# Order and issuing engine of the first loads in a fused spectral-filter and GEGLU kernel

## The chip, the core and the metric

The kernel runs on one core of one Trainium2 chip. The metric is the device time of one execution in microseconds (us); lower is better. Before the change it is 1331.72 us, the median of three runs (1331.66 to 1331.9).

## What is computed

A gate mixes two branches over 2048 tokens of 576 features. Branch A is a 2-D FFT over tokens and features, a product with a complex filter, and the inverse transform. Branch B is a GEGLU layer with 4608 hidden features. All is float32.

```python
x = A_x                                                   # 1 x 2048 x 576
g = sigmoid((x * gate_w).sum(-1, keepdims=True))
a = irfft2(rfft2(x, axes=(-2, -1)) * (w_r + 1j * w_i), s=(2048, 576), axes=(-2, -1))
h = gelu(x @ w_gate, approximate=True) * (x @ w_up)       # 2048 x 4608
b = h @ w_down                                            # 2048 x 576
out = g * a + (1 - g) * b
```

## The kernel before

**Tiling.** The tokens are cut into two halves (p = 0, 1) of 1024, each of two blocks (tb = 0, 1) of 512. The hidden features are 36 tiles of 128 (index j); tile j has a gate part (s = 0) and an up part (s = 1). The 576 input features are contracted in five slices k = 0..4; slice 4 holds the last 64 features twice, in a form of its own. Every float32 product is made of three products of rounded parts: high weight by high x, low weight by high x, high weight by low x. So each slice of x and of the weights is first copied by ScalarE into its high part (the helper `copy`, line 239), and VectorE then subtracts to get the low part. Slice 4 of x needs a copy and two VectorE operations with a mask `msk` (helper `stacked`, lines 243 and 244).

**What order the work has.** The schedule is manual: the instructions of each engine run in the order in which the Python code emits them. Functions `chain` (one tile, one block, one part: 14 matmuls on 512 columns) and `down_mm` (288 columns, the down projection) emit the matmuls; `gap` is called between them and emits a little VectorE and ScalarE work from queues (`aux`, `later`, `gens`), paced by a credit in us. Most of the kernel after the first tiles computes two tiles and two blocks together with seven block products (functions `products` and `seven`, line 1290); the spectral branch runs on VectorE, ScalarE and, for its column transforms, TensorE beside that.

**The start.** Six matmuls on a tile of zeros (`idle`, line 1458) run on TensorE while the first loads are under way. Then `first_chains` (line 879) computes tiles j = 0 and 1 of block tb = 0 together, slice by slice as the loads come in: for k = 0, 1, 2 six matmuls for j = 0 (into `px`) and six for j = 1 (into `pgu`), then slices 4 and 3 of j = 0, then slices 4 and 3 of j = 1. That makes 56 matmuls. After them `chain` runs block tb = 1 of the same two tiles (lines 859 to 866).

The names in the profile: `til<-xt` are loads of x slices, 256 KB each, five for tb = 0 (called xa[0] to xa[4] below; entries 0 to 4 of the list `x0` in the code) and five for tb = 1 (xb[0] to xb[4]; entries 5 to 9 of that list). `low<-wgu` of 128 KB is one slice of the weights of one tile (w0[k] for j = 0, w1[k] for j = 1). `low<-wd` (288 KB) are down weights of one tile. `xraw<-xs` and `tmp<-xs` (256 KB) are quadrants of x for the seven-product part, `rows<-xn` (2304 KB) the rows for the spectral branch and the gate, `low<-gw` the gate vector. `xhi`, `xlo`, `xtl` are the parts of x, `gub` the parts of the gate and up weights, `gl` and `hb` the activations.

**Who asks for what.** SyncE (SP) and GpSimd (POOL) issue the loads. SP asks for the x slices, for w0[0] and w1[0], the mask, xb, the first two down weights, the first four quadrants, the gate vector, the rows and four more quadrants, in this order; POOL asks for the other eight weight slices. Completion of SP's DMAs is counted by eight semaphores used in turn, so each DMA of SP waits until the one eight places ahead of it has landed.

ScalarE's order at the start is: for each k the weight slice of j = 0, the x slice (for k = 0 VectorE makes it), the weight slice of j = 1; then xb[0], xb[1], xb[2]; then the GELU of tile 0 (line 897); then xb[3] and xb[4]; then the GELU of tile 1. VectorE's order follows it: the low parts of xb[0] to xb[2] (line 789), the product of tile 0 (line 904), the low part of xb[3], the two mask operations on xb[4] (lines 243, 244).

```python
for k in (0, 1, 2, 4, 3):
    for j, w in ((0, w0), (1, w1)):
        g = gu_of(j)
        copy(g[:, 0, k], w[:, k])
        ...
        vec.tensor_tensor(g[:, 1, k], w[:, k], f(g[:, 0, k]), ALU.subtract)
        if j == 0 and 0 < k < 4:
            copy(xhi[0][:, k], x0[k])
```

Of the kernel before, what the change touches and what calls it, by code (L numbers as in the profile page):

```python
# [24 lines left out]
KT = 5  # L25
# [150 lines left out]
def _build(nc, tc, a):  # L176
    with ExitStack() as ctx:
# [3 lines left out]
        vec, act, pl, pe = nc.vector, nc.scalar, nc.gpsimd, nc.tensor  # L181

        def mk(n, shape, dt=F32):
            return pool.tile([P] + shape, dt, name=n, tag=n)

        def f(x):
            return x.bitcast(F32)
# [14 lines left out]
        raw = [low[:, i * (KT * 256 + D):(i + 1) * (KT * 256 + D)] for i in range(2)]  # L202
        hb = [mk(f"hb{i}", [2, TB], F32R) for i in range(3)]
        gl = [mk(f"gl{i}", [TB]) for i in range(2)]
        xraw = mk("xraw", [4, TB])
# [6 lines left out]
        msk = mk("msk", [2 + 96])  # L212
# [25 lines left out]
        def copy(o, i):  # L238
            act.activation(o, i, AF.Copy)  # L239
# [546 lines left out]
        def prep_x(tb, k, src):  # L786
            if k < 4:
                copy(xhi[tb][:, k], src)
                vec.tensor_tensor(xlo[tb][:, k], src, f(xhi[tb][:, k]), ALU.subtract)
                credit[0] -= 0.7  # L790
            else:
                copy(xtl[tb], src)
                stacked(xtl[tb], src)
                credit[0] -= 1.45

        def gu_of(j):
            return gub[gu_at(j)].rearrange("p (l t k) -> p l t k", l=2, t=KT)
# [281 lines left out]
        def load_xs(p, i, quads):  # L1079
            for q in range(4):  # L1080
                nc.sync.dma_start(quads[q], a["xs"][p, q // 2, q % 2][:, i])
# [353 lines left out]
        w0, w1 = (raw[j][:, 0:KT * 256].rearrange("p (t k) -> p t k", t=KT) for j in range(2))  # L1435
        w0d, w1d = (a["wgu"][j].rearrange("p (t k) -> p t k", t=KT) for j in range(2))
        for k in (0, 1, 2, 4, 3):
            nc.sync.dma_start(x0[k], a["xt"][0][:, k, 0:TB])
            (pl if k else nc.sync).dma_start(w0[:, k], w0d[:, k])
            (pl if k else nc.sync).dma_start(w1[:, k], w1d[:, k])  # L1440
        nc.sync.dma_start(msk, a["msk"])
        for k in range(KT):
            nc.sync.dma_start(x0[5 + k], a["xt"][0][:, k, TB:2 * TB])
        for i in range(2):
            nc.sync.dma_start(raw[i][:, KT * 256:], a["wd"][i])
        load_xs(0, 0, [xraw[:, q] for q in range(4)])
        nc.sync.dma_start(gwb, a["gw"][0:1, :].to_broadcast([P, D]))
        load_rows(0)
        load_xs(0, 1, [tmp[:, D + TB * q:D + TB * (q + 1)] for q in range(4)])
# [1 line left out]
        idle = hb[2][:, 0]  # L1451
# [4 lines left out]
        ps = ps_gu()  # L1456
        for _ in range(6):
            pe.matmul(ps, idle[:, 0:P], idle, start=True, stop=True)
        for k in (0, 1, 2, 4, 3):
            for j, w in ((0, w0), (1, w1)):  # L1460
                g = gu_of(j)
                copy(g[:, 0, k], w[:, k])
                if j == 0 and k == 0:
                    vec.tensor_copy(xhi[0][:, k], x0[k])
# [3 lines that stand above are left out]
                if j == 0 and k < 4:  # L1468
                    vec.tensor_tensor(xlo[0][:, k], x0[k], f(xhi[0][:, k]), ALU.subtract)
                elif j == 0:  # L1470
                    prep_x(0, k, x0[k])
# [150 lines left out]
```

## Time and profile before

| | |
|---|---|
| time, median of 3 runs | 1331.72 us |
| the profiled execution's own time | 1331.82 us |
| its span, first to last instruction | 1330.1 us |
| TensorE matmul busy | 1320.0 us, 99% of the span |
| VectorE busy | 1163.7 us, 87% |
| ScalarE busy | 873.0 us, 66% |
| GpSimd busy | 277.4 us, 21% |
| mean DMA rate over the span | 186 GB/s |
| DMA rate in the first fortieth of the span (33 us) | 354 GB/s |

Times in the views are us from the start of the span. A line of a timeline gives the start, the length, the engine (PE is TensorE's matmuls, DVE VectorE, ACT ScalarE, SPq the issuing of a DMA by SyncE), the source line, the operation, written and read tile, the count where equal instructions are merged, and in brackets the idle time before it with what ended it. A line of windows gives a stretch, its length, the busy time of each engine with the number of instructions, the granted TensorE clock, the busy share of the 16 DMA engines and the bytes moved in GB/s. In the lines on DMA queues, q1 is the queue of SyncE and q0 that of GpSimd.

### The profile page before, as it was taken

To read this page: it belongs to the slowest core of one execution; us is meant where nothing else is said; L and a number is where in the kernel's file an instruction comes from. 1 tells how busy PE (TensorE), PEld (TensorE's weight loads), DVE (VectorE), ACT (ScalarE), POOL (GpSimd) and SP (SyncE) were. 2 spreads that over 40 slices of the span, in tenths; PEclk is the share of its full clock that TensorE was granted. 3 is DMA by queue.
4 is the path that set the end of the run, shared out by engine and by line. 5 is a ranking of instruction groups with operands and counts; after the bars stand their busy time and mean duration, and the time that the engine had idled before them with its cause. 6 is when DMAs were issued, how large, how long until landed. Compare 5 with 4: busy or idle time off the path is not lost.

```text
span 1330.1 us, 20238 instructions
## 1 busy us (share of the span) xinstructions
PE 1320.0 (99%) x7294; PEld 1167.6 (88%) x7294; DVE 1163.7 (87%) x1653; ACT 873.0 (66%) x1583; POOL 277.4 (21%) x350
## 2 busy tenths in 40 slices
PE   9999999999999999999999999999999999999998
PEld 7888888888888888888888898888888888888887
DVE  7789999978999997975789988899999969999854
ACT  5686765665657557787578787647575686576562
POOL 1011221221212212112302231211222242222241
PEclk9999999999999999999999999999999999999999
DMA  9346677797777777999978998677777798676796
GB/s 354 135 115 128 130 135 136 156 267 164 148 153 139 150 155 183 280 236 287 277 235 214 239 237 193 125 252 220 155 148 147 157 258 179 136 142 127 183 195 178
DMA packets 108693, 247.57 MB, mean 186 GB/s; under 512 B 12848, under 2 KB 17840, under 8 KB 106800
## 3 DMA queue, kind: packets, MB, share of 16 engines
q0 software_dynamic: 46752, 97.34, 44.4%
q1 hardware_dynamic: 61840, 148.93, 34.1%
q8 instruction: 57, 0.93, 0.3%
q14 instruction: 44, 0.36, 0.1%
HBM read 133.88 MB, written 109.95 MB: 183 GB/s over the span
## 4 chain that ended last, share of the span: by engine, by line
PE 95%; ACT 2%; DVE 1%; issue 1%; DMA 0%; SPq 0%; DVEq 0%; ACTq 0%
PE pdn L943 33%; PE px L1290 20%; PE pgu L1290 20%; PE px L1292 3%; PE pgu L1292 3%; PE pgu L859 3%; PE pgu L860 3%; PE pgu L861 3%; PE pdn L304 1%; PE px L304 1%; ACT til L239 1%; PE px L860 1%; PE px L861 1%; PE px L859 1%; PE pgu L865 1%; PE pgu L866 1%
## 5 line engine op out<-in xcount | busy, mean ns | idle before, releaser
L956 POOL DMA_DIRECT2D yd<-stg x264 | 226.8, 862 | 953.8 <-ACT stg L975 894.3
L975 ACT ACTIVATE stg<-pdn,omg 128x576 f32<-128x576 f32 x276 | 204.8, 743 | 334.8 <-PE pdn L943 203.8
L943 PE MATMUL pdn<-dn,hb 128*128 128x288 f32 x1572 | 231.1, 294 | 0.1
L943 PEld LDWEIGHTS pdn<-dn,hb 128*128 128x128 f32 x1572 | 221.7, 188 | 9.5 <-ACT stg L975 0.7
L1277 DVE TENSOR_TENSOR gub<-low,gub 128x768 fp32r<-128x768 f32 x124 | 118.2, 953 | 8.4 <-ACT gub L1274 7.0
L1290 PE MATMUL pgu<-xhi,gub 128*128 128x512 f32 x392 | 122.0, 392 | 0.6 <-ACT px L239 0.6
L1290 PE MATMUL pgu<-til,gub 128*128 128x512 f32 x420 | 107.4, 391 | 0.0
L943 PE MATMUL pdn<-dn,ext 128*128 128x288 f32 x672 | 106.7, 294 | 0.0
L943 PE MATMUL pdn<-dn,gub 128*128 128x288 f32 x672 | 106.5, 294 | 0.0
L239 ACT ACTIVATE gub<-low 128x512 fp32r<-128x512 f32 (+2 forms) x147 | 97.7, 666 | 13.4 <-DVE low L1267 6.4
L943 PEld LDWEIGHTS pdn<-dn,ext 128*128 128x128 f32 x672 | 98.0, 188 | 4.1
L943 PEld LDWEIGHTS pdn<-dn,gub 128*128 128x128 f32 x672 | 97.8, 188 | 4.0
L1290 PEld LDWEIGHTS pgu<-til,gub 128*128 128x128 f32 x420 | 77.0, 188 | 14.5
L1290 PE MATMUL px<-xhi,gub 128*128 128x512 f32 x280 | 86.9, 391 | 0.0
L1290 PE MATMUL px<-til,gub 128*128 128x512 f32 x336 | 86.0, 391 | 0.0
L1290 PEld LDWEIGHTS pgu<-xhi,gub 128*128 128x128 f32 x392 | 70.8, 188 | 13.3 <-ACT px L239 1.1
L943 PE MATMUL pdn<-dn,hx 128*128 128x288 f32 x516 | 82.3, 296 | 0.0
L1267 DVE TENSOR_TENSOR low<-low 128x768 f32<-128x768 f32 x81 | 77.3, 955 | 0.8
L1290 PE MATMUL pgu<-xlo,gub 128*128 128x512 f32 x196 | 76.3, 389 | 0.0
L859 PE MATMUL pgu<-xhi,gub 128*128 128x512 f32 x192 | 75.1, 391 | 0.0
L860 PE MATMUL pgu<-xhi,gub 128*128 128x512 f32 x192 | 75.0, 391 | 0.0
L861 PE MATMUL pgu<-xlo,gub 128*128 128x512 f32 x192 | 74.9, 390 | 0.0
(278 smaller groups left out, 2968.9 us busy)
## 6 DMA issues: line engine op xcount, KB each, us to landing
yd<-stg POOLq DMA_DIRECT2D x264, 288.0 KB, 5.1
low<-ws SPq DMA_DIRECT2D x94, 384.0 KB, 4.8
gub<-wd SPq DMA_DIRECT2D x56, 288.0 KB, 3.9
low<-wgu SPq DMA_DIRECT2D x13, 640.0 KB, 7.1
rows<-col POOLq DMA_DIRECT2D x32, 256.0 KB, 5.9
gub<-ws SPq DMA_DIRECT2D x18, 384.0 KB, 5.2
lo<-dn SPq DMA_DIRECT2D x18, 288.0 KB, 2.7
dn<-lo POOLq DMA_DIRECT2D x18, 288.0 KB, 5.1
```

Source lines behind the costliest of these rows:

```text
L239: act.activation(o, i, AF.Copy)
L304: pe.matmul(v[al][:, :NK], c[:, al, q], two(x)[:, al], start=n == 0, stop=n == 2)
L859: pe.matmul(ps, w[:, 0, k, c], xhi[tb][:, k], start=k == 0, stop=False)
L860: pe.matmul(ps, w[:, 1, k, c], xhi[tb][:, k], start=False, stop=False)
L861: pe.matmul(ps, w[:, 0, k, c], xlo[tb][:, k], start=False, stop=False)
L943: pe.matmul(ps[half], h[:, l, c], d[:, q, half * HD:(half + 1) * HD], start=part == 0 and n == 0, stop=part == 1 and n == 2)
L956: pl.dma_start(yd[u], o, accum_op=ALU.add)
L975: at(n, lambda: put(u, lambda o: act.activation(o.rearrange("p (c k) -> p c k", c=2), v[:, :, 0:HD], AF.Copy, scale=omg[:, u:u + 1]), i == 0))
L1267: vec.tensor_tensor(o, p, q, ALU.subtract)
L1277: vec.tensor_tensor(w[:, 0:5:2], x, f(w[:, 1:4]), ALU.subtract)
L1290: pe.matmul(ps, l, x[:, t], start=first and t == 0 and q == 0, stop=False, skip_group_check=True)
L1292: pe.matmul(ps, w[:, 512 + P * s:512 + P * (s + 1)], xt, start=False, stop=True, skip_group_check=True)
```

## The change

Only the first loads change. SP now asks for the whole of what tiles 0 and 1 of block tb = 0 need, slice by slice: xa[k], w0[k], w1[k] for k = 0, 1, 2, then the mask, then slices 4 and 3; after them the xb slices, the gate vector, the rows and the second four quadrants. GpSimd no longer asks for weight slices. It sets 16 columns of the tile of zeros to zero once more, which makes it wait until the six matmuls on that tile have read it, and then asks for the two down weights and the first four quadrants, which SP asked for before. No instruction of TensorE, VectorE or ScalarE is added, removed or moved.

```diff
         for k in (0, 1, 2, 4, 3):
             nc.sync.dma_start(x0[k], a["xt"][0][:, k, 0:TB])
-            (pl if k else nc.sync).dma_start(w0[:, k], w0d[:, k])
-            (pl if k else nc.sync).dma_start(w1[:, k], w1d[:, k])
-        nc.sync.dma_start(msk, a["msk"])
+            nc.sync.dma_start(w0[:, k], w0d[:, k])
+            nc.sync.dma_start(w1[:, k], w1d[:, k])
+            if k == 2:
+                nc.sync.dma_start(msk, a["msk"])
         for k in range(KT):
             nc.sync.dma_start(x0[5 + k], a["xt"][0][:, k, TB:2 * TB])
-        for i in range(2):
-            nc.sync.dma_start(raw[i][:, KT * 256:], a["wd"][i])
-        load_xs(0, 0, [xraw[:, q] for q in range(4)])
         nc.sync.dma_start(gwb, a["gw"][0:1, :].to_broadcast([P, D]))
         load_rows(0)
         load_xs(0, 1, [tmp[:, D + TB * q:D + TB * (q + 1)] for q in range(4)])
 ...
         ps = ps_gu()
         for _ in range(6):
             pe.matmul(ps, idle[:, 0:P], idle, start=True, stop=True)
+        pl.memset(f(idle)[:, 0:16], 0.0)
+        for i in range(2):
+            pl.dma_start(raw[i][:, KT * 256:], a["wd"][i])
+        for q in range(4):
+            pl.dma_start(xraw[:, q], a["xs"][0, q // 2, q % 2][:, 0])
```

In SP's program (the queue of DMA issues of SyncE from its start), the first rows before are these; `til` from `xt` with 128x512 is an x slice, `low` from `wgu` with 128x256 a weight slice:

```order
L1438 DMA til_69<-xt 128x512
L1439 DMA low<-wgu 128x256
L1440 DMA low<-wgu 128x256
L1438 DMA til_69<-xt 128x512 x4
L1441 DMA msk<-msk 128x98
L1443 DMA til_69<-xt 128x512 x4
L1443 DMA til_70<-xt 128x512
L1445 DMA low<-wd 128x576 x2
L1081 DMA xraw<-xs 128x512 x4
L1447 DMA low<-gw 128x576
```

SP's program after the change reads like this from the third x slice to the first four of xb:

```order
L1438 DMA til_69<-xt 128x512
L1439 DMA low<-wgu 128x256
L1440 DMA low<-wgu 128x256
L1442 DMA msk<-msk 128x98
L1438 DMA til_69<-xt 128x512
L1439 DMA low<-wgu 128x256
L1440 DMA low<-wgu 128x256
L1438 DMA til_69<-xt 128x512
L1439 DMA low<-wgu 128x256
L1440 DMA low<-wgu 128x256
L1444 DMA til_69<-xt 128x512 x4
```

The second x slice keeps its place, the fourth in the program. The eight weight slices have come in between the x slices, so the third x slice is now the seventh DMA instead of the fifth, and the first of xb the 17th instead of the ninth. The down weights and quadrants between xb and the gate vector are gone.

GpSimd's program before, from its first DMA on, has eight weight slices, one memset and then the first accumulating store:

```order
L1439 DMA low<-wgu 128x256
L1440 DMA low<-wgu 128x256
L1439 DMA low<-wgu 128x256
L1440 DMA low<-wgu 128x256
L1439 DMA low<-wgu 128x256
L1440 DMA low<-wgu 128x256
L1439 DMA low<-wgu 128x256
L1440 DMA low<-wgu 128x256
L690 MEMSET rows 128x512
L956 DMA yd_109<-stg_87 128x576
```

At the same place after the change stand these rows (`hb_83` is the tile of zeros):

```order
L690 MEMSET rows 128x512
L1457 MEMSET hb_83 128x16
L1459 DMA low<-wd 128x576 x2
L1461 DMA xraw<-xs 128x512 x4
L956 DMA yd_109<-stg_87 128x576
```

The weight slices have left; behind the memset of `rows` come the small memset that waits for the six matmuls, two down weights and four quadrants.

## The prediction

> **What bounds the kernel now.** I read the page's busy times and chain first, then TensorE's waits over the whole span, then the timelines of the first 20 us. Page:
>
> ```profile
> PE 1320.0 (99%) x7294; PEld 1167.6 (88%) x7294; DVE 1163.7 (87%) x1653; ACT 873.0 (66%) x1583; POOL 277.4 (21%) x350
> PE 95%; ACT 2%; DVE 1%; issue 1%; DMA 0%; SPq 0%; DVEq 0%; ACTq 0%
> ```
>
> TensorE is busy 99% of the span and is 95% of the chain that ended last. A change that leaves TensorE's instructions alone can only win back its idle time or add to it. These are all its waits (us in total, times, longest):
>
> ```profile
> PE pdn L304 <- ACT stg L975: 1.8, 2, 1.3
> PE pgu L1458 <- DVE gate L1454: 1.5, 1, 1.5
> PE px L860 <- DVE gub L831: 1.1, 1, 1.1
> PE pgu L1290 <- ACT px L239: 0.6, 1, 0.6
> PE px L879 <- ACT xhi L239: 0.4, 1, 0.4
> ```
>
> The sum is 5.4 us. The first, third and fourth lie at lines of the later stages, and the second is the start. Only the last, at line 879, is in the first chains, where this change works. TensorE's timeline there:
>
> ```profile
> 1.45 2.93 PE L1458 MATMUL pgu<-hb 128*128 128x512 f32 x6 [1.45 <-DVE gate L1454]
> 6.86 1.08 PE L879 MATMUL pgu<-xhi,gub 128*128 128x512 f32 x4
> 8.84 1.20 PE L879 MATMUL px<-xhi,gub 128*128 128x512 f32 x4 [0.43 <-ACT xhi L239]
> 9.87 0.63 PE L879 MATMUL px<-xlo,gub 128*128 128x512 f32 x2
> 11.71 1.07 PE L879 MATMUL px<-xhi,gub 128*128 128x512 f32 x4
> 13.07 1.07 PE L879 MATMUL pgu<-xhi,gub 128*128 128x512 f32 x4
> 13.98 0.62 PE L879 MATMUL pgu<-xlo,gub 128*128 128x512 f32 x2
> 18.97 0.39 PE L859 MATMUL px<-xhi,gub 128*128 128x512 f32 x1
> 21.69 0.39 PE L865 MATMUL px<-xtl,gub 128*128 128x512 f32 x1
> ```
>
> Six matmuls take 1.36 us once things run (11.71 to 13.07), and four take 0.91 (13.07 to 13.98). The six for slice 0 of tile 1 begin at 6.86 and would be followed at 8.22; slice 1 begins at 8.84, so 0.62 us are lost. The next four take 1.03 us (8.84 to 9.87) instead of 0.91: another 0.12. That is 0.74 us, and behind it the row of matmuls has no wait until block tb = 1 at 18.97. What ended it, on ScalarE:
>
> ```profile
> 3.78 0.42 ACT L239 ACTIVATE gub<-low 128x256 fp32r<-128x256 f32 x1 [1.55 <-DMA low<-wgu]
> 8.16 0.63 ACT L239 ACTIVATE xhi<-til 128x512 fp32r<-128x512 f32 x1 [1.42 <-DMA til<-xt]
> 12.74 2.01 ACT L239 ACTIVATE xhi<-til 128x512 fp32r<-128x512 f32 x3
> ```
>
> The copy at 8.16 is that of xa[1]; it waited for the load. The chain of waits has the same load, and SP's queue and GpSimd show when each was asked for:
>
> ```profile
> 2.12 6.01 DMA til<-xt
> 0.74 0.39 SPq L1438 DMA_DIRECT2D til<-xt  x1
> 2.12 1.86 SPq L1438 DMA_DIRECT2D til<-xt  x4
> 1.29 0.71 POOL L1439 DMA_DIRECT2D low<-wgu  x1 [0.84 <-POOLq L1608]
> 5.19 0.55 POOL L1440 DMA_DIRECT2D low<-wgu  x1
> DMA to landing us min/median/max: 2.7/6.7/8.2
> ```
>
> xa[0], asked for at 0.74, took 2.7 us (the minimum); xa[1], asked for at 2.12, took 6.01. Between them GpSimd's weight slices and SP's later x slices share the 16 engines. The stretches show how full these are:
>
> ```profile
> 1.75:3.25 1.50, 1.50 (x4) 1.19 (x4) 0.00 (x0) 0.47 (x2) 1.50 (x4) 1.00 0.89 264
> 3.25:4.75 1.50, 1.50 (x4) 0.83 (x3) 0.95 (x3) 0.42 (x1) 1.50 (x4) 1.00 0.70 160
> 4.75:9.50 4.75, 4.32 (x15) 3.09 (x14) 1.95 (x5) 2.07 (x6) 1.52 (x3) 1.00 1.01 361
> 9.50:14.00 4.50, 4.50 (x22) 3.69 (x21) 3.70 (x10) 4.41 (x10) 0.00 (x0) 1.00 1.04 386
> ```
>
> There is a thin stretch of 160 GB/s, as GpSimd's first transfers come in, and from 4.75 on the engines are full. So from there on the order of the bytes decides, and whatever goes forward pushes something back.
>
> **The change, part by part.**
>
> *xa[1] and the weights of slice 1.* xa[1] stays SP's fourth DMA, asked for at 2.12. Ahead of it on the wire are only xa[0], w0[0] and w1[0]; with itself that is 256+128+128+256 KB = 0.79 MB. At the rows' rates 0.40 MB have passed by 3.25 (1.5 us at 264 GB/s); the other 0.39 MB take 1.1 us at 361 GB/s or 2.4 us at 160, so they have passed at 4.3 or 5.7. From passing to landing I take 0.7 us from xa[0]: its 0.26 MB at 264 GB/s from 1.75 end at 2.75, and it landed at 3.44. xa[1] lands at 5.0 to 6.4. TensorE wants it at 8.22; in the trace its matmuls began 0.68 us after the copy (8.16 to 8.84), so it must be there by 7.5. Both ends hold. The two weight slices behind it (0.26 MB) pass 0.7 us later at 361 GB/s. The gap goes: -0.74 us.
>
> *SP's issue time.* SP now issues 16 DMAs before xb instead of eight. One takes about 0.46 us (1.86 for four): the last weight slice is asked for near 8 us. Slice 3 is wanted at 8.22 + 4 x 1.36 + 0.91 = 14.6. SP's wait for the DMA eight places ahead adds nothing as long as those land in under 8 x 0.46 = 3.7 us. Cost nothing; cover about 3 us.
>
> *GpSimd.* Its small memset waits until the six matmuls end (4.38). Behind it on its engine stand only the six DMAs; the first accumulating stores come far later. It issues from about 4.5 to 8 (0.71 + 5 x 0.55). The down weights and quadrants come to SBUF sooner than before. Cost nothing in itself.
>
> *What is pushed back: xb.* SP's bytes up to and with xb[2] are 8 x 256 + 10 x 128 + 49 KB = 3.46 MB, before and after. But 2 x 288 + 4 x 256 KB = 1.64 MB of down weights and quadrants came behind xb, and now run beside it from GpSimd's queue. Call X the time at which xb[2] has landed. Before, the third of the three copies at 12.74 began at 12.74 + 2.01 - 0.63 = 14.1. By the stretches' rates 3.46 MB had passed at 12.4, so the lag to landing had grown to 1.7 us. What hangs on X is in order on two engines:
>
> ```profile
> 17.30 0.69 DVE L904 TENSOR_TENSOR gl<-gl,px 128x512 f32<-128x512 f32 x1 [0.40 <-ACT gl L897]
> 17.91 0.69 DVE L789 TENSOR_TENSOR xlo<-til,xhi 128x512 fp32r<-128x512 f32 x1
> 18.51 0.48 DVE L243 TENSOR_SCALAR til<-til,msk 128x512 f32<-128x512 f32 x1
> 19.03 0.75 DVE L244 SCALAR_TENSOR_TENSOR xtl<-xtl,msk,til 128x512 fp32r<-128x512 f32 x1
> ```
>
> After X come, by the starts of these rows, the copy (0.65 with the hand-over), the low part (0.60 until the next can start), the product of tile 0 (0.61), the low part of xb[3] (0.60), and the two mask operations (0.52 and 0.75): xb[4] is ready at X + 3.8. The matmul that reads it, line 865, ran at 21.69; without the gap it would run at 20.95. So X up to 17.2 costs nothing, every us beyond costs one, and at X = 17.9 the whole gain is gone. The wait would come once: afterwards both engines' next results for TensorE are some us early.
>
> X from both sides. By the rows 0.40 + 0.24 + 1.71 + 1.74 = 4.09 MB pass until 14.0. If all of GpSimd's 1.64 MB goes ahead of xb[2], 5.10 MB pass at 14.0 + 1.01/0.386 = 16.6, and with a lag of 1.7 us X = 18.3. If the thin stretch does not recur (it cost (361 - 160) x 1.5 = 0.30 MB, 0.8 us), X = 17.5. For the other side, these are the queues' shares before, with both queues filled, from 5.5 to 7.5 and from 7.5 to 9.5:
>
> ```profile
> q1 hardware_dynamic: 310, 0.57, 75.7%
> q0 software_dynamic: 67, 0.19, 25.5%
> ...
> q1 hardware_dynamic: 211, 0.36, 54.1%
> q0 software_dynamic: 133, 0.37, 50.9%
> ```
>
> GpSimd's queue took 0.19 of 0.76 MB, then 0.37 of 0.73. Its data will begin to flow near 6.5, an estimate: two us after its first issue, twice the 1.0 us from SP's first issue at 0.74 to the stretch from 1.75. By then SP has moved about 1.57 MB without it (0.40 plus 3.25 us at 361 GB/s); 1.89 MB of the 3.46 are left. At 75% of 386 GB/s they pass at 13.0 and X = 14.7; at half, GpSimd's bytes are through at 15.0, SP's at 15.6, and X = 17.3; at the mean of the two stretches (62%) X = 16.1. I take X between 16 and 17.4, near the mean row, and so a cost of 0 to 0.2 us.
>
> [...]
>
> *Slices 4 and 3* run in the same contest: through w0[3] SP has 2.49 MB to move, 0.92 left at 6.5; at half of 386 GB/s they pass at 11.3, with 1.7 us lag at 13.0, and copies of 0.42 and 0.63 us make it 14.1 against 14.6. No cost, cover 0.5 us.
>
> Sum: -0.74 + 0.1 = -0.6 us on the profiled execution's own 1331.82, so 1331.2; that execution lies 0.10 above the median of the runs, so I forecast **1331.1 us** for the median, 0.05% less than 1331.72.
>
> **Rivals.**
>
> *The gap stays.* If the thin stretch belongs to the first x and weight loads themselves and not to the meeting of two queues, and is longer or thinner without GpSimd, xa[1] lands after 7.5. For it: the engines were only 70% busy at 3.25 to 4.75 while transfers were asked for. Against it: even at 160 GB/s it lands at 6.4. The time is then 1331.7. [...] The trace shows 2.7 us against 6.01 for two equal loads, so what is ahead on the wire counts.
>
> *Slower: the mask operation on xb[4] takes the gap's place.* GpSimd's 1.64 MB goes ahead of xb, a thin stretch comes as its queue starts, and X = 18.3: a wait of 1.1 us at line 865, net +0.4, 1332.1. It decides from X = 17.9. For it: GpSimd's share rose to half once its queue was full, and xb moves from ninth to 17th. Against it: the 75% row.
>
> *Slower by far: the late backlog.* SP's issue order behind xb is the same, with the weights of tile 2 behind the rows. VectorE makes their low part, and TensorE reads them, here:
>
> ```profile
> 32.63 1.49 DVE L831 TENSOR_TENSOR gub<-low,gub 128x1280 fp32r<-128x1280 f32 x1
> 38.03 0.40 PE L859 MATMUL px<-xhi,gub 128*128 128x512 f32 x1
> ```
>
> That is 3.9 us of cover. The bytes ahead are the same as before, so I see no slip of that size; at 7 us of slip the time would be 1334 or more.
>
> **How the numbers follow.** 0.2% is 2.7 us, about what a measurement of this kernel can tell from no change. The forecast case (gap gone, cost 0 to 0.3) has 0.62: 1330.9 to 1331.3. Part of the gain given back (X from 17.5 to 17.9), 1331.3 to 1331.7: 0.13. The gap stays: 0.07. The mask operation late: 0.12. The backlog, or another stall of over 2.7 us: 0.05. A gain of over 2.7 us has no source in the waits above: 0.01. The lower end is a full -0.74 and the spread of the runs (0.24): 1330.7. The upper end is the second rival's: 1332.1. So faster 0.01, same 0.94, slower 0.05.
>
> **What would show it.** Right: line 879 has no wait for `xhi`, slice 1 of TensorE starts near 8.2, tb = 1 near 18.2, and line 865 follows its chain without a pause. X shows in the three copies of xb on ScalarE: the third begins before 17.2. Wrong: the copy of xa[1] still after 7.5 (first rival), or TensorE waiting on VectorE's line 244 at line 865 (second rival), or any wait longer than 2.7 us in the first 60 us, or GpSimd's issues taking much longer than 0.55 us each.

## Result and the profile after

The changed kernel takes 1335.37 us (median of six runs, 1334.4 to 1338.2); the kernel before, in the same session, 1331.86 (six runs, 1331.66 to 1332.54). The ratio is 1.003, 95% interval 1.002 to 1.004. The forecast was 1331.1, its range 1330.7 to 1332.1: the kernel became slower where no measurable change was forecast. The profiled execution took 1335.35 us, its span 1333.6 (1330.1 before), so the trace holds the whole difference, 3.5 us.

All of it lies in the first 23 us; TensorE's waits after them are those of the kernel before. TensorE's timeline of the changed kernel:

```profile
7.91 0.63 PE L879 MATMUL pgu<-xlo,gub 128*128 128x512 f32 x2
8.38 1.08 PE L879 MATMUL px<-xhi,gub 128*128 128x512 f32 x4
12.47 1.07 PE L879 MATMUL pgu<-xhi,gub 128*128 128x512 f32 x4
13.37 0.61 PE L879 MATMUL pgu<-xlo,gub 128*128 128x512 f32 x2
16.09 1.16 PE L879 MATMUL px<-xtl,gub 128*128 128x512 f32 x4 [2.10 <-DVE xtl L244]
17.34 2.07 PE L879 MATMUL px<-xhi,gub 128*128 128x512 f32 x4
19.21 1.05 PE L879 MATMUL px<-xlo,gub 128*128 128x512 f32 x2
20.07 1.32 PE L879 MATMUL pgu<-xtl,gub 128*128 128x512 f32 x4
22.60 0.39 PE L859 MATMUL px<-xhi,gub 128*128 128x512 f32 x1
```

The gap before slice 1 is gone: its matmuls start at 8.38, right behind those of slice 0. Slice 4, which the two matmuls at 13.37 (0.46 us as they are spaced) would have been followed by at 13.83, starts at 16.09: 2.26 us lost. From there the 20 matmuls of slices 4 and 3 take 22.60 - 16.09 = 6.51 us; before they took 18.97 - 14.43 = 4.54. Block tb = 1 therefore starts at 22.60 instead of 18.97, 3.63 us later. The terms: the gap -0.74, a start that is 0.12 slower (6.98 against 6.86 for tile 1's first matmuls), the wait +2.26, the slow matmuls +1.97; together 3.61.

What the wait hangs on stands in ScalarE's timeline of the same kernel (the copies of slices 4 and 3) and in its chain of waits (start, length, what):

```profile
6.61 0.61 ACT L239 ACTIVATE xhi<-til 128x512 fp32r<-128x512 f32 x1
9.48 0.42 ACT L239 ACTIVATE gub<-low 128x256 fp32r<-128x256 f32 x1
13.70 0.42 ACT L239 ACTIVATE gub<-low 128x256 fp32r<-128x256 f32 x1 [3.80 <-DMA low<-wgu]
16.35 0.42 ACT L239 ACTIVATE gub<-low 128x256 fp32r<-128x256 f32 x1 [0.48 <-DMA low<-wgu]
17.50 1.84 ACT L239 ACTIVATE xhi<-til 128x512 fp32r<-128x512 f32 x3
```

```profile
2.12 3.81 DMA til<-xt
7.87 8.45 DMA low<-wgu
```

ScalarE sat 3.80 us until w0[4] had landed at 13.68. The mask operations on xa[4], which VectorE runs behind the low part of w0[4] as the code orders them, released TensorE at 16.09; VectorE is named in TensorE's wait, but what had held VectorE up was the load of w0[4], asked for at 5.94 and landed 7.74 us later. In the chain, xa[1] takes 3.81 us instead of 6.01, and its place is taken by w0[3], asked for at 7.87 and landed 8.45 us later, at 16.32.

Why a load of 128 KB takes 7.74 or 8.45 us is read from the stretches and from the queues' shares of the changed kernel:

```profile
3.25:4.75 1.50, 1.50 (x4) 0.76 (x3) 0.88 (x3) 0.42 (x1) 0.31 (x2) 1.00 0.77 177
6.50:8.00 1.50, 1.50 (x7) 1.19 (x7) 1.17 (x3) 1.03 (x3) 1.39 (x3) 1.00 0.95 309
8.00:9.50 1.50, 1.50 (x8) 1.23 (x7) 0.71 (x2) 0.95 (x3) 0.00 (x0) 1.00 1.04 276
9.50:14.00 4.50, 4.49 (x20) 3.38 (x18) 1.03 (x2) 0.70 (x2) 0.00 (x0) 1.00 1.01 383
...
17.00:20.50 3.50, 3.41 (x10) 2.49 (x9) 3.05 (x6) 2.91 (x7) 0.00 (x0) 0.52 1.10 396
```

From 6.5 on the DMA engines were busy all the time (the last column but one is 0.95 to 1.10), so it is a question of whose bytes passed. These are the queues (packets, MB, share of the engines' time) from 0 to 6.5, from 6.5 to 14, SP's from 6.5 to 15, and then both from 12.5 to 13.5 us with the packets by size:

```profile
q1 hardware_dynamic: 1006, 1.30, 65.8%
...
q0 software_dynamic: 470, 1.62, 61.1%
q1 hardware_dynamic: 930, 0.98, 39.6%
...
q1 hardware_dynamic: 1219, 1.33, 46.8%
...
DMA packets 187, 0.40 MB, mean 404 GB/s; under 512 B 30, under 2 KB 92, under 8 KB 187
q0 software_dynamic: 89, 0.29, 74.0%
q1 hardware_dynamic: 98, 0.11, 32.0%
```

By 14.0 GpSimd's queue had moved 1.62 of its 1.64 MB, and SP's in the same 7.5 us only 0.98 MB of what TensorE was waiting for: 38%. Between 12.5 and 13.5 it was 0.11 of 0.40 MB, 27%. There the packets show how. Below 512 B are 30 small ones, the mask having passed by then; 62 more are below 2 KB, rows of 1 KB of the weight slices (128 KB over 128 partitions). GpSimd's 0.29 MB went in 71 packets of 4 KB, two rows of 2 KB in each. SP's other 24 are rows of xa[3], 2 KB each. So 86 packets of SP passed beside 71 of GpSimd: 1.2 to one by count, and a quarter of the bytes. The counts are this near to each other late in the contest only. From 9.5 to 10.5 us the trace has, packets of 4 bytes left out, 91 rows of SP (mostly of 2 KB) against 46 packets of GpSimd, two to one and 0.16 of 0.36 MB; from 8 to 9.5, with 101 rows of the mask among SP's, it is 165 against 61. Why SP's count was the higher early on is not shown.

In these traces SP's packets have the size of a row of the load (1024 B for a weight slice, 2048 B for an x slice), and GpSimd's are longer than its rows. In the kernel before, GpSimd asked for the same weight slices, and the trace has their rows of 1 KB in 256 packets of 4096 B, four rows to a packet. So the change also took these weights (1.05 MB) from 256 packets of 4096 B to 1024 of 1024 B.

The last row of the stretches shows the second loss: from 17.0 to 20.5 us the granted clock was 0.52. By the trace's records it was at half from 17.12 to 20.54. Of the 1.97 us on slices 4 and 3, 0.34 are a second wait (the four matmuls at 16.09 are followed at 17.34 instead of 17.00: w0[3], landed at 16.32, and xa[3] behind it in ScalarE's order), and the other 1.6 are the clock.

### The profile page after: what moved, and what is told of

It reads as the page before. It is cut to its first block, busy times and chain, and to the rows that moved or that the text cites. A ratio compares the mean times of both kernels' runs of the same rounds, so it can differ in the third digit from the quotient of the medians.

```text
span 1333.6 us, 20237 instructions
## 1 busy us (share of the span) xinstructions
PE 1321.9 (99%) x7294; PEld 1168.6 (88%) x7294; DVE 1164.2 (87%) x1653; ACT 873.1 (65%) x1583; POOL 275.6 (21%) x349
## 4 chain that ended last, share of the span: by engine, by line
PE 95%; ACT 2%; DMA 1%; DVE 1%; issue 1%; SPq 0%; DVEq 0%; ACTq 0%
PE pdn L943 33%; PE px L1290 20%; PE pgu L1290 20%; PE px L1292 3%; PE pgu L1292 3%; PE pgu L859 3%; PE pgu L860 3%; PE pgu L861 3%; PE pdn L304 1%; PE px L304 1%; ACT til L239 1%; PE px L860 1%; PE px L861 1%; PE px L859 1%; PE pgu L865 1%; PE pgu L866 1%
```

## Experiments

My theory after the result had two parts. First, the loss is GpSimd's early traffic: its large packets take turns with SP's small rows (71 beside 86 from 12.5 to 13.5 us), and so the weights of slices 4 and 3 come late, while the order on SP's queue is by itself a gain. Second, TensorE's idle time then let the clock fall (0.52 from 17.0 to 20.5 us), which makes up 1.6 of the 3.5 us. The rivals: SP's issuing of sixteen DMAs one after the other is what makes slices 4 and 3 late; or the bytes alone count, whatever the rows. Where times are compared with the kernel before, it ran in the same sessions at 1331.49 to 1331.63. The changed kernel ran in the first session only, 3.5 above the kernel before, so a comparison with it is fairer by that difference than by the medians.

**The order on SP alone (e1_sp_all).** GpSimd's part is taken out, SP asks for its loads behind xb as it did before.

```diff
+        for i in range(2):
+            nc.sync.dma_start(raw[i][:, KT * 256:], a["wd"][i])
+        load_xs(0, 0, [xraw[:, q] for q in range(4)])
         nc.sync.dma_start(gwb, a["gw"][0:1, :].to_broadcast([P, D]))
...
-        pl.memset(f(idle)[:, 0:16], 0.0)
-        for i in range(2):
-            pl.dma_start(raw[i][:, KT * 256:], a["wd"][i])
-        for q in range(4):
-            pl.dma_start(xraw[:, q], a["xs"][0, q // 2, q % 2][:, 0])
```

> Order alone: SP asks for the first weights and x slices in order of use, as in the changed kernel, and then itself, behind xb, for the down weights and quadrants, as before; GpSimd asks for nothing. Theory (GpSimd's queue took the engines' turns from SP's weight slices): w0[4] lands near 9 instead of 13.7, TensorE has no wait at slices 4 and 3, block tb = 1 begins near 18.2, and the time is 1331.1 us, 0.7 below before. Rival (16 loads issued by SP alone, each waiting for the one eight places ahead, are too slow): SP's issues are the same as in the changed kernel, so w0[4] stays near 13.7 and the time near 1335.

Measured: 1330.68 us (11 runs, 1330.08 to 1331.49), ratio to before 0.9995 (0.9986 to 1.0004). Its median is 0.9 below that of before, with an interval that just includes no change, and 4.7 below that of the changed kernel. TensorE's timeline:

```profile
7.67 1.20 PE L879 MATMUL px<-xhi,gub 128*128 128x512 f32 x4 [0.17 <-ACT xhi L239]
12.79 0.61 PE L879 MATMUL pgu<-xlo,gub 128*128 128x512 f32 x2
13.24 1.07 PE L879 MATMUL px<-xtl,gub 128*128 128x512 f32 x4
17.77 0.39 PE L859 MATMUL px<-xhi,gub 128*128 128x512 f32 x1
```

SP issues the same sixteen DMAs at the same pace, and slice 4 follows slice 2 without a pause; w0[4] landed at 9.51. The rival of SP's issuing falls. The loss comes with GpSimd's part. (That tb = 1 starts 1.20 us earlier than in the kernel before overstates the gain: in this execution tile 1's first matmuls already start at 5.95 instead of 6.86, behind four matmuls on data that took 1.23 us instead of 2.07.)

**GpSimd's part alone (e6_pool_part).** The first weight slices stay as in the kernel before, and GpSimd asks for the down weights and quadrants behind them.

```diff
-            nc.sync.dma_start(w0[:, k], w0d[:, k])
-            nc.sync.dma_start(w1[:, k], w1d[:, k])
-            if k == 2:
-                nc.sync.dma_start(msk, a["msk"])
+            (pl if k else nc.sync).dma_start(w0[:, k], w0d[:, k])
+            (pl if k else nc.sync).dma_start(w1[:, k], w1d[:, k])
+        nc.sync.dma_start(msk, a["msk"])
```

> The other part alone: the first weights are asked for by GpSimd as in the kernel before, and behind them GpSimd, not SP, asks for the down weights and quadrants, with the small memset. Theory: these wait in GpSimd's own queue behind its weight slices, so slices 4 and 3 come as before; only SP's xb (rows of 2 KB against 4 KB) meets them and gets a third of the engines, so xb[2] lands at 16 to 17 instead of 14.1, before the 17.9 at which the mask operation on xb[4] would hold up TensorE. The time stays within 0.5 of 1331.7. Rival (GpSimd's loads beside SP's cost as much anywhere): 1334 or more.

Measured: 1332.31 (10 runs, 1331.79 to 1332.87), ratio 1.0006 (0.9997 to 1.0016); tb = 1 starts at 19.68 instead of 18.97. The third copy of xb began at 18.51, later than I expected, but TensorE does not wait at line 865. The 0.7 us arise earlier: slice 1 starts at 9.12 instead of 8.84, and slice 4 at 14.95 instead of 14.43, behind the mask, which landed at 13.40 instead of 12.10. Queues from 14 to 16 us, where SP's rows are those of xb, 2 KB each:

```profile
DMA packets 305, 0.78 MB, mean 391 GB/s; under 512 B 47, under 2 KB 47, under 8 KB 305
q0 software_dynamic: 151, 0.51, 66.6%
q1 hardware_dynamic: 154, 0.27, 38.1%
```

Of the 258 packets that are not small, 0.27 MB in rows of 2 KB make some 130, and the rest, 0.51 MB in packets of 4 KB, some 125: near equal counts again, and 35% of the bytes. The two parts do not add up: the order alone -0.9, GpSimd's part alone +0.8 (each with an interval that includes no change), both +3.5. Only together do they put the weights of slices 4 and 3 into the contest in 1 KB rows, behind 1.6 MB of SP's own bytes.

**Half the dose (e4_wd_only).** GpSimd asks only for the two down weights; the quadrants go back to SP behind xb.

```diff
+        load_xs(0, 0, [xraw[:, q] for q in range(4)])
         nc.sync.dma_start(gwb, a["gw"][0:1, :].to_broadcast([P, D]))
...
-        for q in range(4):
-            pl.dma_start(xraw[:, q], a["xs"][0, q // 2, q % 2][:, 0])
```

> The changed kernel with GpSimd asking for the two down weights only (0.59 MB); the four quadrants go back to SP behind xb. Theory: GpSimd's queue is empty from about 10.5 on instead of 14.5, SP has the engines to itself again, w0[4] lands near 11.5 instead of 13.7, the wait at slice 4 falls from 2.3 us to 0.3 and the clock does not fall, and the time is 1331.0 to 1331.5. Rival (any use of GpSimd's queue there costs the same, by its start): 1335.

Measured: 1331.56 (10 runs, 1330.89 to 1331.92), ratio 1.0002 (0.9992 to 1.0011). TensorE at slice 4, and the stretch behind it:

```profile
12.79 0.61 PE L879 MATMUL pgu<-xlo,gub 128*128 128x512 f32 x2
14.33 1.17 PE L879 MATMUL px<-xtl,gub 128*128 128x512 f32 x4 [0.92 <-ACT xhi L239]
15.34 1.08 PE L879 MATMUL px<-xhi,gub 128*128 128x512 f32 x4
```

```profile
14.00:20.00 6.00, 5.67 (x25) 4.72 (x26) 5.93 (x12) 5.03 (x11) 0.00 (x0) 1.00 1.00 340
```

With 0.59 MB instead of 1.64 from GpSimd, w0[4] landed at 11.91 and slice 4 waits 14.33 - 13.24 = 1.09 us, more than the 0.3 I expected: from the landing of w0[4] to the first matmul of slice 4 pass 2.42 us here and 2.41 in the changed kernel, with the copies on ScalarE and the low part and both mask operations on VectorE between them. The clock kept 1.00. So the loss goes with GpSimd's bytes, and an idle time of 1.09 us did not cost the clock.

**Keeping TensorE busy (e3_filler).** The changed kernel, with nine matmuls on zeros between slices 2 and 4, in a bank that nothing reads.

```diff
+                if (j, k) == (0, 4):
+                    v = ps_dn()
+                    for _ in range(9):
+                        pe.matmul(v[:, 0], hb[2][:, 0, 0:P], hb[2][:, 0], start=True, stop=True)
```

> The changed kernel with nine more matmuls on zeros (2.0 us at full clock, into an unused part of PSUM) between slices 2 and 4 of the first chains, where TensorE sat idle 2.3 us. Theory (the idle time made the clock fall to half for 3.4 us, which cost about 1.7 us on top of the wait): the clock stays full until the end, slices 4 and 3 run at 0.23 us a matmul, and the time falls by 1.7 to 1333.7. Rival (the slow matmuls come from late operands, not from the clock): no change, 1335.4.

Measured: 1333.94 (10 runs, 1333.62 to 1335.37), ratio 1.002 (1.0011 to 1.0029), 1.4 below the changed kernel, or 1.1 when each is taken against the kernel before of its own session. TensorE's timeline, and the stretch that was at 0.52:

```profile
13.55 2.24 PE L879 MATMUL pdn<-hb 128*128 128x512 f32 x9
16.76 1.18 PE L883 MATMUL px<-xtl,gub 128*128 128x512 f32 x4 [0.97 <-DVE xtl L244]
17.78 1.09 PE L883 MATMUL px<-xhi,gub 128*128 128x512 f32 x4
21.44 0.39 PE L859 MATMUL px<-xhi,gub 128*128 128x512 f32 x1
```

```profile
17.00:20.50 3.50, 3.50 (x16) 2.79 (x16) 3.30 (x7) 3.50 (x8) 0.00 (x0) 1.00 1.13 364
```

The weights are no earlier (w0[4] landed at 14.35, and slice 4 starts at 16.76), but the clock stays full (1.00 from 17.0 to 20.5 us), and the 20 matmuls take 21.44 - 16.76 = 4.68 us instead of 6.51. That shows the second part of the theory in the trace. The medians point the same way, work without use making the kernel some 1.1 to 1.4 us faster, though the two intervals (1.002 to 1.004 and 1.0011 to 1.0029) overlap.

**GpSimd later (e5_late_pool).** GpSimd's block moves behind the splitting of the weights, and a small memset that writes into the raw w0[3] makes it wait until that has been read.

```diff
-        pl.memset(f(idle)[:, 0:16], 0.0)
...
+        pl.memset(w0[:, 3, 0:16], 0.0)
+        for i in range(2):
+            pl.dma_start(raw[i][:, KT * 256:], a["wd"][i])
+        for q in range(4):
+            pl.dma_start(xraw[:, q], a["xs"][0, q // 2, q % 2][:, 0])
```

> The changed kernel, but GpSimd's small memset writes into the raw weights of slice 3 of tile 0 instead of the tile of zeros, so that it and the six loads behind it wait until slice 3 has been split. Theory (GpSimd's queue beside SP's weight slices is the cause): GpSimd begins near 12, slices 4 and 3 and xb land as without it, the down weights and quadrants land by 19 to 20, and the time is 1331.1. Rival (SP's issue): 1335.

Measured: 1336.38 (5 runs, 1336.26 to 1338.05), ratio 1.004 (1.0028 to 1.0053): a miss by five us. The first chains run as in the order alone (tb = 1 at 17.66), but now GpSimd's loads, issued from 12.95 on, are late. TensorE at its first down projection, then the queues from 18 to 22 us:

```profile
27.18 1.48 PE L943 MATMUL pdn<-dn,hb 128*128 128x288 f32 x10
33.00 3.56 PE L943 MATMUL pdn<-dn,hb 128*128 128x288 f32 x14 [4.34 <-DVE hb L928]
```

```profile
q1 hardware_dynamic: 78, 1.44, 83.6%
q0 software_dynamic: 70, 0.28, 17.1%
```

Here the bytes go the other way. SP's queue has come to the rows for the spectral branch, 18 KB each (2304 KB over 128 partitions): 78 packets against 61 (nine of GpSimd's 70 are of 4 bytes), but 1.44 MB against 0.28. Shares by bytes alone would not turn round like this, so that rival falls too. The quadrants are late, VectorE waits for them (2.21 us before its additions at line 1090), its product `hb` at line 928 stands behind these in its order, and TensorE waits 4.34 us for that, after which the granted clock from 33.0 to 36.5 was 0.54.

**Longer rows (e2_rows3k, e2b_rows3k_whole).** If the row's size sets the share, the weights of slices 2 to 4 fetched in rows of 3 KB should come sooner. In the first kernel each tile's load is cut by partitions, in the second it is whole.

```diff
+        for j in range(2):
+            for r in (slice(0, 32), slice(32, 64), slice(64, P)):        # e2_rows3k
+                nc.sync.dma_start(raw[j][r, 512:KT * 256], a["wgu"][j][r, 512:])
...
+        for j in range(2):                                               # e2b_rows3k_whole
+            nc.sync.dma_start(raw[j][:, 512:KT * 256], a["wgu"][j][:, 512:])
```

> The changed kernel with GpSimd's loads as they are, but SP's weight slices 2, 3 and 4 of a tile are fetched together, in rows of 3 KB instead of three rows of 1 KB, cut by partitions into three DMAs so that the number of SP's DMAs stays 16. Theory (the engines take turns by packet, and a row of SP's is one packet against about 4 KB of GpSimd's): after 7.5 us SP has 512 rows left before xb instead of 1024, so xa[3] lands near 12 instead of 16, the wait at slice 4 falls from 2.3 us to under 0.5, and the time is 1331 to 1332. Rival (turns by bytes, SP getting the same 130 GB/s): 0.97 MB are left instead of 1.10, xa[3] lands near 14.5, the wait stays over 1 us and the time near 1333 to 1334. Rival of the issue: 1335.

Measured: 1337.12 (5 runs, 1336.57 to 1338.83), ratio 1.0042 (1.0029 to 1.0056).

> As the run with rows of 3 KB, but each of the two loads covers all 128 partitions at once (12 instead of 16 DMAs before xb). In that run the engines together moved only 250 GB/s from 7.5 to 14 us, which I put down to the loads of 32 and 64 partitions. Theory (turns by packet, one row of SP's to 4 KB of GpSimd's): the rate stays near 380 GB/s, SP gets about 40% of it, xa[3] lands near 12 to 13, the waits at slices 2 to 4 sum to under 1 us, and the time is 1331 to 1332. Rival (turns by bytes, or GpSimd's queue simply first): SP gets 130 GB/s as in the changed kernel, xa[4] lands near 13 and xa[3] near 15, and the time is 1334 or more.

Measured: 1335.79 (5 runs, 1334.7 to 1337.44), ratio 1.0033 (1.002 to 1.0046). Both times miss. The stretch from 9.5 to 12 of the first, and for the second the queues from 9.5 to 10.5 and slice 2 on TensorE:

```profile
9.50:12.00 2.50, 1.85 (x9) 1.19 (x7) 0.00 (x0) 0.00 (x0) 0.00 (x0) 1.00 1.02 258
```

```profile
q0 software_dynamic: 63, 0.25, 62.3%
q1 hardware_dynamic: 81, 0.14, 38.1%
```

```profile
12.71 2.07 PE L879 MATMUL px<-xhi,gub 128*128 128x512 f32 x4 [1.93 <-ACT xhi L239]
```

In the first, the engines moved only 258 GB/s with a busy share of 1.02: the cut loads were slow, so the run says nothing on the share. In the second SP's share was 0.14 of 0.39 MB, 36%. That says little on rows of 3 KB: 31 of SP's 74 rows in this stretch are short ones of the mask, and the changed kernel had 0.16 of 0.36 MB from 9.5 to 10.5. The weights of slice 2 are now part of a load three times as long, and TensorE waits 1.93 us at 12.71, a stall that the changed kernel does not have there. The longer rows and the joining of three slices into one load are not told apart in the time. So no run here changes the row's size alone.

**The mask's rows (e7_mask_first, e8_mask_twice).** The mask is 49 KB in 128 rows of 392 B. If each row takes a turn, as in the theory, it costs as much of the contest as 128 rows of any size. In one kernel it moves ahead of the contest, behind w1[0]; in the other a second copy goes behind the first.

```diff
-            if k == 2:
+            if k == 0:                                                   # e7_mask_first
                 nc.sync.dma_start(msk, a["msk"])
...
+                nc.sync.dma_start(tmp[:, 0:98], a["msk"])                # e8_mask_twice
```

> The changed kernel with one of SP's loads moved: the mask (49 KB, 128 rows of 392 bytes) is asked for behind w1[0] instead of behind w1[2], so that it has passed before GpSimd's transfers begin. Theory (one row of SP's is one turn, however short): in the changed kernel SP got about 50 rows through in each half us of the contest, so 128 rows fewer bring w0[4] 1.3 us earlier, at 12.4 instead of 13.7; the wait at slice 4 falls from 2.3 to 1.0 us and the clock probably stays up, so the time is 1332.4 to 1334.1. Rival (shares by bytes): 49 KB at 130 GB/s are 0.4 us, w0[4] lands at 13.3 and the time is 1335.0.

Measured: 1334.8 (10 runs, 1333.62 to 1336.42), ratio 1.0023 (1.0014 to 1.0032).

> The changed kernel with the mask loaded twice, the second time into unused columns of another tile, one behind the other: 49 KB and 128 rows more ahead of xa[4]. Theory (one row, one turn): w0[4] lands about 1.0 us later, near 14.7 (part of the rows passes after GpSimd's queue is empty), and the time is 1336.4. Rival (bytes): 0.4 us, 1335.75.

Measured: 1336.61 (4 runs, 1336.48 to 1337.65), ratio 1.0039 (1.0025 to 1.0053). Slice 4 on TensorE in the second:

```profile
17.91 2.05 PE L879 MATMUL px<-xtl,gub 128*128 128x512 f32 x4 [3.67 <-DVE xtl L244]
```

With another 128 rows slice 4 starts at 17.91 instead of 16.09, and the median is 1.2 us higher (1.5 by sessions), though 49 KB are 0.13 us of the 383 GB/s. That alone would agree with shares by count of rows. Taking the rows out of the contest brought 0.6 (0.3 by sessions) and not the 1.3 or more expected, inside both kernels' spread. In its trace w0[4] landed at 15.11, later than the 13.68 of the changed kernel and close to the 15.50 with the mask twice; that execution is the slowest of its ten runs (1336.42) and does not stand for the median, but it shows that w0[4] can shift by 1.4 us without more rows. The pair does not settle the theory.

**A version faster than both (e9_dve_cast).** The order alone still left a wait of 0.17 us at slice 1 (0.44 by the pace of the matmuls), for ScalarE's copy of xa[1]. Here, in addition, VectorE makes that copy.

```diff
-                if j == 0 and k == 0:
+                if j == 0 and k < 2:
...
-                if j == 0 and 0 < k < 4:
+                if j == 0 and 1 < k < 4:
```

> The order-only kernel (SP asks for everything, first slices in order of use), and the high part of xa[1] is made by VectorE's cast (0.43 us, as for xa[0]) instead of ScalarE's copy (0.62 us, behind the copy of w0[1]). In the order-only run TensorE still waited 0.44 us at slice 1 for that copy, with xa[1] landed 0.7 us before it began. Theory: the wait goes, tb = 1 begins near 17.4 in a run with the same clock start, and the time is 1330.3, 0.4 below the order-only kernel and 1.2 below before. Rival (w0[1], which lands last, holds slice 1): no change against the order-only kernel, 1330.7.

Measured: 1330.39 (11 runs, 1330.11 to 1330.68), ratio 0.9991 (0.9982 to 0.9999), 1.2 below before. Slice 1 follows without a wait:

```profile
7.01 0.63 PE L879 MATMUL pgu<-xlo,gub 128*128 128x512 f32 x2
7.48 1.08 PE L879 MATMUL px<-xhi,gub 128*128 128x512 f32 x4
```

## Why the prediction was wrong

- **What bounds the kernel** held: TensorE is 99% busy before and after, and only its idle time and its clock moved.
- **xa[1]** held: landed at 5.92 (forecast 5.0 to 6.4), copy at 6.61, gap gone. The first rival, that the gap stays, did not happen, though its premise did: the thin stretch came again, 177 GB/s, with no packet of GpSimd yet.
- **SP's issue time** held: the last weight slice was asked for at 8.75 (forecast near 8), and the order alone shows that it costs nothing.
- **GpSimd** held on times (issues from 4.49 to 7.9) but not on "Cost nothing in itself".
- **xb** was sized too favourably: xb[2] landed at 18.68, where I took 16 to 17.4, and beyond the 18.3 that I had as the far end. It cost nothing here, because TensorE came to line 865 late for another reason; so the second rival did not decide. No run shows the cost of 0.1 us that my sum has: in e6_pool_part too, with the third copy at 18.51, TensorE did not wait at line 865.
- **Slices 4 and 3** is the step that failed: "0.92 left at 6.5; at half of 386 GB/s they pass at 11.3, with 1.7 us lag at 13.0 ... No cost, cover 0.5 us". Two of its terms were mis-sized. SP had moved 1.30 MB by 6.5, not 1.57, since I had left the thin stretch out of this step; the 0.27 MB more that were left are 1.4 us at half of 386 GB/s. (The mask's 0.05 MB, ahead of slices 4 and 3, I had left out too.) SP's share was 38%, not half, and the mean rate from 6.5 to 14.0 was 2.60 MB in 7.5 us, 347 GB/s: 0.13 MB/us instead of 0.19. So the 2.49 MB had passed near 14.6 (2.28 by 14.0, 2.63 by 15.0) instead of 11.3. The lag of 1.7 us held: w0[3] landed at 16.32 instead of 13.0. The step also priced only slice 3, with 1.05 us of copies. Slice 4 comes first, and it follows the landing of w0[4] by 2.41 us, so for no wait at 13.83 w0[4] had to land by 11.42; it landed at 13.68 (9.51 in e1_sp_all, 11.91 in e4_wd_only). I had priced xb at four shares, from 75% to nothing, and the nearer victim at one.
- **The clock** had no term at all. Of the 3.5 us, 1.6 are the half clock that followed the stall of 2.26 us; so "or another stall of over 2.7 us" (0.05 of chance) was in fact a stall of 2.26 that grew.

I had priced the contest by halves of the bytes, and the bytes went 27 to 73 in one stretch (12.5 to 13.5 us of the changed kernel) and 84 to 16 in another (18 to 22 us of e5_late_pool). The counts of packets were nearer to each other there, 86 against 71 and 78 against 61. In other stretches they were not: 91 against 46 in the changed kernel from 9.5 to 10.5 us, and from 5.5 to 7.5 us in the kernel before, where the prediction's row has 75.7%, 277 rows of SP against 46 packets of GpSimd, though GpSimd had asked for the last of its slices at 5.19. What held GpSimd's queue back there stays open, so the size of a share is argued from counts and not shown; that GpSimd's transfers took it from SP's weights is shown by e1_sp_all and e4_wd_only.

The half-speed stretch of the changed kernel lasted 3.42 us (17.12 to 20.54), and the timeline has 2.10 us of idle time in brackets ahead of it. The two runs with rows of 3 KB have shorter waits. These are a stretch of e2b_rows3k_whole, behind its 1.93 us of idle time before 12.71, and a wait and a stretch of e2_rows3k:

```profile
12.00:15.00 3.00, 2.29 (x5) 1.82 (x6) 1.73 (x4) 1.39 (x4) 0.00 (x0) 0.62 1.03 396
```

```profile
13.00 1.20 PE L879 MATMUL px<-xhi,gub 128*128 128x512 f32 x4 [1.65 <-ACT xhi L239]
```

```profile
15.00:18.00 3.00, 1.67 (x6) 0.98 (x6) 0.76 (x2) 0.89 (x3) 0.00 (x0) 1.00 1.04 381
```

In the first the clock was 0.62 in this stretch and 0.81 in the next (15 to 18 us); at half, that is 3.4 us from 12.7 on. That of the second was 1.00 from 9.5 to 18 us, through the wait of 1.65 us and one of 1.36. So in these traces the half clock came behind 2.10 and 1.93 us of idle time and not behind 1.65 (nor 0.92 in e4_wd_only and 0.97 in e3_filler). What sets the fall and its length is not shown.

Open, too: why the rate was 309 and 276 GB/s from 6.5 to 9.5 us with the engines busy. Rows of 392 B and packets of GpSimd fall there together, but the mask's place and number changed little: from 4.75 to 9.5 us the rate was 321 in the changed kernel, 327 with the mask moved ahead and 329 with the mask twice.

## What to carry to other kernels

When two queues are full, count packets beside bytes: here SP's loads, mostly in 1 KB rows beside a queue in 4 KB packets, got down to 27% of the bytes at 86 packets to 71. Price every load that is still to come in that contest by the packets that the trace has for its queue, the one that is needed first before all and up to the instruction that uses it, and do not fill a second queue with what is needed later while the first carries what is needed now. Here a stall of TensorE of 2.26 us was followed by 3.42 us at half clock, 1.6 us of time, so a forecast needs a term for that.

## What the runs showed of the hardware

- SP's share of the bytes beside GpSimd's packets of 4 KB or more, in three stretches: 27% with mostly 1 KB rows (changed kernel, 12.5 to 13.5 us, 86 packets to 71), 35% with 2 KB (e6_pool_part, 14 to 16 us, some 130 to 125), 84% with 18 KB (e5_late_pool, 18 to 22 us, 78 to 61). In others two to six of SP's packets went to one: 91 to 46 and 165 to 61 in the changed kernel (9.5 to 10.5 and 8 to 9.5 us), 277 to 46 before (5.5 to 7.5 us).
- In the traces of the kernels before and after, SP's packets in the first 30 us have the size of one row of their load (392 B for the mask, 1024 B, 2048 B, up to 18,432 B for the rows), and GpSimd's hold several: 256 packets of 4096 B for 1 KB rows before; 256 of 4096 B for 2 KB rows and 128 of 4608 B for rows of 2304 B after.
- A granted clock of half for 3.4 us behind 2.10 us of idle time on TensorE in the changed kernel, about 1.6 us of time lost, and behind 1.93 us in e2b_rows3k_whole; none behind 1.65 us in e2_rows3k.
- A thin stretch at 3.25 to 4.75 us in six traces, also with SP's queue alone: 160 GB/s before, 177 after the change, 151 in e1_sp_all, 156 in e9_dve_cast, 175 in e7_mask_first, 168 in e8_mask_twice.
- Loads of 32 and 64 partitions in 3 KB rows, beside GpSimd's queue (e2_rows3k), with all engines at 258 GB/s and a busy share of 1.02 from 9.5 to 12 us; uncut loads of the same rows (e2b_rows3k_whole) at 394 in that stretch.
- The first four matmuls on data took 1.23 us in e1_sp_all and 2.07 and 2.08 before and after, behind the same six matmuls (2.92 and 2.93 us). The trace's records have the clock at full from 6.70 us before and from 6.88 after. So single executions differ by the better part of a microsecond from this alone, and medians of many runs are what small effects here have to be read from.
